# The last 64 rows of two weight matrices as whole rows on 64 partitions

## The chip, the cores and the metric

The kernel runs on one core of one Trainium2 chip. The metric is the time of one execution on the device in microseconds (us). Three executions of the kernel before took 196.46, 196.88 and 197.08 us; the median is 196.88 us. A further execution was taken with the hardware profiler; all durations of instructions and transfers below are from that one.

## The reference

Two branches read the same input x (8 rows of 448) and are mixed by a gate:

```python
q = x @ wq                                  # 8 x 448 times 448 x 4096: 16 heads of 256
scores = q . k * 256**-0.5                  # 8 KV heads, the last 1024 of 4096 cached keys
o = softmax(scores) . v                     # two query heads share one KV head
a = o @ wo                                  # 4096 x 448

y = layernorm(x)
b = gelu(y @ w1 + b1) @ w2 + b2             # 448 -> 1792 -> 448

g = sigmoid((x * gate_w).sum(-1))
out = g * a + (1 - g) * b
```

All tensors are bf16. The keys and values that are read come to 64 MiB; the weights wq, wo, w1 and w2 come to about 10 MiB.

## The kernel before

**Layout of the weights.** The contraction length of wq and w1 is 448 = 3 x 128 + 64. The first 384 rows lie in `wq_sb` and `w1_sb` as three slices of 128 partitions. The last 64 rows (DM to D) lie in `wq_t` and `w1_t` (lines 109 and 112) on all 128 partitions: each row is cut into two halves, and row r's half h lies on partition 2r + h. One partition then holds 4096 B of wq or 1792 B of w1.

Since a partition of these tiles holds only one half of a row, the transposed input must be zero on the partitions of the other half. `halves` (line 261) copies the last 64 columns of x (or y) into every second column of a zeroed tile `x_e` (or `y_e`), once per half, and `transposed` (line 268) turns the three slices and the two halves over on TensorE: five transposes, one copy to `xT` or `yT` with five slices of 8 columns.

**The MLP's first product** (`mlp_up`, line 311) makes 14 blocks of 128 outputs by 8. A block is five matmuls into one PSUM range: three with `w1_sb` (line 321), one with a single row `b1_sb` against ones, which adds the bias (line 325), and one with `w1_t` (line 329). The products for q (line 377) are 96 matmuls with `wq_sb` and 32 with `wq_t`.

**Transfers.** SyncE's queue (SP) issues, in this order, w1 (1344 KB), the tail of w1 (224 KB), w2 (1568 KB), three slices of wq (1024 KB each), the tail of wq (512 KB), and then the stream of K, V and wo: 1024 KB for two batch rows of one KV head, 448 KB for the wo rows of one head. ScalarE's queue (ACT) issues x, b1 and b2 at the start and gate_w later. There are eight semaphores for transfers, used in rotation over both queues, so that a transfer is issued only when the transfer eight places before it has landed whole. K and V have twelve buffers.

**Order.** The order of instructions is the program's own. After the MLP and q, a loop over 64 steps (two per K transfer) transposes the K tile on TensorE (line 407), copies it out of PSUM on VectorE (line 412), multiplies with q (line 433), and, seven steps behind, multiplies the exponentials with V (line 508). The last steps are the V products of the last head, the product with the last wo tile (line 533), the mix (line 577) and two transfers of the output.

Of the kernel before, what the change touches and what calls it, by code (L numbers as in the profile page):

```python
# [9 lines left out]
ALU = mybir.AluOpType  # L10
AXIS = mybir.AxisListType
BF16 = mybir.dt.bfloat16
F32 = mybir.dt.float32
# [3 lines left out]
def kernel(  # L17
# [15 lines left out]
    nc = tc.nc  # L33
    P = nc.NUM_PARTITIONS

    B, Sq, D = A_x.shape
    _, Hkv, Sk, Dh = A_k_cache.shape
    HD = A_wq.shape[1]
    Hq = HD // Dh
    rep = Hq // Hkv  # L40
    W = min(4096, max(256, Sk // 4))
    kv0 = Sk - W
    F = B_w1.shape[1]
    NB = B
    NJ = Dh // P
    TB = 2
    NC = W * TB // P
    HC = NC // TB
    NF = F // P
    R = NB * rep  # L50
    RU = TB * rep
    NBU = NB // TB
    DC = D // P
    DM = DC * P
    TL = D - DM
    HH = HD // 2
    assert Sq == 1 and Dh % P == 0 and W % P == 0 and F % P == 0
    FH = F // 2
    NH = NF // 2
    assert TL * 2 == P and NC * R <= 2 * P and NB % TB == 0 and 3 * 32 <= P and R <= 32 and NF % 2 == 0  # L60
    qscale = float(Dh) ** -0.5
    NU = NBU * Hkv
    NSTEP = NU * TB
# [8 lines left out]
    PT = CP * CT  # L72
    DN = D // CT
# [14 lines left out]
    big = ctx.enter_context(tc.tile_pool(name="big", bufs=1))  # L88
    kvpool = ctx.enter_context(tc.tile_pool(name="kvpool", bufs=NKV))
    ktpool = ctx.enter_context(tc.tile_pool(name="ktpool", bufs=3))  # L90
    consts = ctx.enter_context(tc.tile_pool(name="consts", bufs=1))
    work = ctx.enter_context(tc.tile_pool(name="work", bufs=2))
    ps_kt = ctx.enter_context(
        tc.tile_pool(name="ps_kt", bufs=4, space=bass.MemoryType.PSUM)
    )
# [10 lines left out]
    big.tile([P, PAD], BF16, name="pad")  # L106
    NKH = rep * NJ
    wq_sb = big.tile([P, DC, HD], BF16, name="wq_sb")
    wq_t = big.tile([P, HH], BF16, name="wq_t")
    w1_sb = big.tile([P, DC, F], BF16, name="w1_sb")  # L110
    wo_sb = [big.tile([P, NKH, D], BF16, name=f"wo_sb{g}") for g in range(Hkv)]
    w1_t = big.tile([P, FH], BF16, name="w1_t")
    w2_sb = big.tile([P, NF, D], BF16, name="w2_sb")
    x_sb = consts.tile([NB, D], BF16, name="x_sb")
    gw_sb = consts.tile([NB, D], BF16, name="gw_sb")
    b1_sb = consts.tile([1, F], BF16, name="b1_sb")
    b2_sb = consts.tile([1, D], BF16, name="b2_sb")
    ident = consts.tile([P, P], BF16, name="ident")
    identf = consts.tile([P, P], F32, name="identf")
    onesb = consts.tile([P, P], BF16, name="onesb")  # L120
# [3 lines left out]
    cross = consts.tile([TB, TB, rep], BF16, name="cross")  # L124
    diag = [consts.tile([P, R], BF16, name=f"diag{k}") for k in range(2)]
    qT = consts.tile([P, NJ, Hkv, NB, rep], BF16, name="qT")
    xT = consts.tile([P, DC + 2, NB], BF16, name="xT")
    yT = consts.tile([P, DC + 2, NB], BF16, name="yT")
    x_e = consts.tile([NB, 2, P], BF16, name="x_e")
    y_e = consts.tile([NB, 2, P], BF16, name="y_e")  # L130
    gg = consts.tile([NB, 2], F32, name="gg")
    gg4 = consts.tile([PT, 2], F32, name="gg4")
    bvec = consts.tile([PT, DN], F32, name="bvec")
    bsum = consts.tile([PT, DN], F32, name="bsum")
    res = consts.tile([PT, DN], BF16, name="res")

# [4 lines left out]
    def load(kind, n):  # L141
# [11 lines left out]
            )  # L153
        KV[kind, n] = t

    nc.scalar.dma_start(x_sb[:], xf)
    nc.scalar.dma_start(b1_sb[:], B_b1.rearrange("(o f) -> o f", o=1))
    nc.scalar.dma_start(b2_sb[:], B_b2.rearrange("(o d) -> o d", o=1))
    nc.sync.dma_start(  # L159
        w1_sb[:], B_w1[0:DM, :].rearrange("(p c) n -> p c n", c=DC)  # L160
    )
    nc.sync.dma_start(w1_t[:], B_w1[DM:D, :].rearrange("r (h n) -> (r h) n", h=2))  # L162
    w2_v = w2_sb[:].rearrange("p (h k) n -> p h k n", h=2)
    nc.sync.dma_start(w2_v, B_w2.rearrange("(h p k) n -> p h k n", h=2, k=NH))  # L164
    wq_v = A_wq[0:DM, :].rearrange("(p c) n -> p c n", c=DC)
    for c in range(DC):
        nc.sync.dma_start(wq_sb[:, c, :], wq_v[:, c, :])  # L167
    nc.sync.dma_start(wq_t[:], A_wq[DM:D, :].rearrange("r (h n) -> (r h) n", h=2))

    VU = (SPG + LAG) // TB  # L170
    units = []
# [47 lines left out]
    )  # L219
    for t in diag:  # L220
        nc.gpsimd.memset(t[:], 0.0)
    nc.gpsimd.memset(x_e[:], 0.0)
    nc.gpsimd.memset(y_e[:], 0.0)
    nc.gpsimd.tensor_copy(identf[:], ident[:])
    sel = consts.tile([NB, PT], F32, name="sel")
    nc.gpsimd.tensor_copy(
# [5 lines left out]
    prod = consts.tile([NB, D], F32, name="prod")  # L232
# [7 lines left out]
    y_sb = consts.tile([NB, D], BF16, name="y_sb")  # L240
# [7 lines left out]
        op0=ALU.subtract, op1=ALU.mult,  # L248
# [3 lines left out]
    A_ps = A_bank[0:PT, 0:DN]  # L252
# [4 lines left out]
        rhs=zrow[:].unsqueeze(1).to_broadcast([1, 512 // P, P]),  # L257
        start=True, stop=True, skip_group_check=True,
    )

    def halves(dst, src):
        for h in range(2):
            nc.vector.tensor_copy(
                dst[:, h, :].rearrange("b (r h) -> b r h", h=2)[:, :, h],
                src[:, DM:D],
            )

    def transposed(dst, t, t_e):
        v = t[:, 0:DM].rearrange("b (p c) -> b c p", c=DC)
        parts = [v[:, c, :] for c in range(DC)] + [t_e[:, h, :] for h in range(2)]  # L270
        tp = ps_kt.tile([P, W], BF16, tag="ktp", name="tp")
        for c, part in enumerate(parts):
            nc.tensor.transpose(
                tp[:, c * NB : (c + 1) * NB], part, ident[0:NB, 0:NB]
            )
        nc.vector.tensor_copy(
            dst[:], tp[:, 0 : len(parts) * NB].rearrange("p (c b) -> p c b", b=NB)
        )

    halves(y_e, y_sb)  # L280
    transposed(yT, y_sb, y_e)
    halves(x_e, x_sb)
    transposed(xT, x_sb, x_e)


    def gate_load():
        src = gate_w.rearrange("(o d) -> o d", o=1)
        nc.scalar.dma_start(gw_sb[:], src.to_broadcast([NB, D]))

    def gate():  # L290
        nc.vector.tensor_tensor(prod[:], x_sb[:], gw_sb[:], op=ALU.mult)
        nc.vector.reduce_sum(gsum[:], prod[:], axis=AXIS.X)
        nc.scalar.activation(gth[:], gsum[:], ACT.Tanh, scale=0.5)
        nc.vector.tensor_scalar(
            gg[:, 0:1], gth[:], 0.5, 0.5, op0=ALU.mult, op1=ALU.add
        )
        nc.vector.tensor_scalar(
            gg[:, 1:2], gg[:, 0:1], -1.0, 1.0, op0=ALU.mult, op1=ALU.add
        )

        nc.tensor.matmul(
            A_bank[0:PT, DN : DN + 2], lhsT=sel[:], rhs=gg[:],
            start=False, stop=True, skip_group_check=True,
        )
        nc.vector.tensor_copy(gg4[:], A_bank[0:PT, DN : DN + 2])
        nc.vector.tensor_scalar_mul(bvec[:], bsum[:], gg4[:, 1:2])


    M = {}
# [1 line left out]
    def mlp_up():  # L311
        h_ps = ps_g.tile([P, 512], F32, tag="grp", name="h_ps")
        for h in range(2):
            for k in range(NH):
                o = h_ps[:, (h * NH + k) * NB : (h * NH + k + 1) * NB]

                def cols(w):
                    return w.rearrange("p (q k) -> p k q", k=NH)[:, k, :]

                for c in range(DC):  # L320
                    nc.tensor.matmul(  # L321
                        o, lhsT=cols(w1_sb[:, c, h * FH : (h + 1) * FH]),
                        rhs=yT[:, c, :], start=(c == 0), stop=False,
                    )
                nc.tensor.matmul(
                    o, lhsT=cols(b1_sb[:, h * FH : (h + 1) * FH]),
                    rhs=onesb[0:1, 0:NB], start=False, stop=False,
                )
                nc.tensor.matmul(  # L329
                    o, lhsT=cols(w1_t[:]), rhs=yT[:, DC + h, :],  # L330
                    start=False, stop=True,
                )
        N = NF * NB
        z = consts.tile([P, N], F32, name="z")
        u = consts.tile([P, N], F32, name="u")
        th = consts.tile([P, N], F32, name="th")
        hT = consts.tile([P, N], BF16, name="hT")
        nc.vector.tensor_copy(z[:], h_ps[:, 0:N])  # L338
        nc.vector.tensor_tensor(u[:], z[:], z[:], op=ALU.mult)
        nc.vector.tensor_scalar(u[:], u[:], 0.044715, 1.0, op0=ALU.mult, op1=ALU.add)  # L340
        nc.vector.tensor_tensor(u[:], u[:], z[:], op=ALU.mult)
        nc.scalar.activation(th[:], u[:], ACT.Tanh, scale=0.7978845608028654)
        nc.vector.tensor_scalar(th[:], th[:], 1.0, 0.5, op0=ALU.add, op1=ALU.mult)
        nc.vector.tensor_tensor(hT[:], th[:], z[:], op=ALU.mult)  # L344
        M["hT"] = hT
# [23 lines left out]
    NQ = Hq * NJ  # L369
    for c in range(DC + 1):  # L370
        for k in range(NQ):
            if c < DC:
                w, xs = wq_sb[:, c, k * P : (k + 1) * P], xT[:, c, :]
            else:
                h, kk = divmod(k, NQ // 2)
                w, xs = wq_t[:, kk * P : (kk + 1) * P], xT[:, DC + h, :]
            nc.tensor.matmul(
                q_ps[:, k * NB : (k + 1) * NB],
                lhsT=w,
                rhs=xs,  # L380
                start=(c == 0 and k == 0),
                stop=(c == DC),
                skip_group_check=True,
            )
# [161 lines left out]
    for n in range(LAST):  # L546
# [28 lines left out]
    o_proj(Hkv - 1)  # L575

    nc.vector.scalar_tensor_tensor(  # L577
        res[:], in0=A_ps, scalar=gg4[:, 0:1], in1=bvec[:], op0=ALU.mult, op1=ALU.add
    )
    for j, eng in enumerate((nc.sync, nc.scalar)):  # L580
        eng.dma_start(
# [30 lines left out]
```

## Time and profile before

| what | value |
|---|---|
| median of three executions | 196.88 us |
| the profiled execution's own time | 196.92 us |
| its span, first to last instruction | 195.2 us |
| TensorE, VectorE, ScalarE, GpSimd busy | 164.2, 113.1, 6.4, 2.8 us |
| moved by DMA | 78.14 MB, mean 400 GB/s |
| packets on SP's queue (q1), share of 16 DMA engines over the span | 12688, 95.4% |
| packets on ACT's queue (q10) | 52 |
| packets that bring instructions (q8) | 26 of 16 KB |
| mean granted TensorE clock | 0.768 |

The device time of an execution is some 1.7 us longer than the span, which runs from the first to the last instruction of the program. In lists of groups, `L407 PE MATMUL ktp<-ident,kv x1024` is line 407, engine, operation, the tile written and the tiles read, and the count; PEld is TensorE's weight load. `SPq` and `ACTq` are the queues' issuing instructions. In the windows view the last two numbers of a line are the share of time that the 16 DMA engines were moving packets, and the GB/s.

### The profile page before, as it was taken

What the parts mean: (1) busy time and instruction counts of PE and PEld (TensorE: products, weight loads), DVE (VectorE), ACT (ScalarE), POOL (GpSimd) and SP (SyncE); (2) the same over time, 40 slices, a digit from 0 to 9 for tenths busy, and PEclk for the clock granted to TensorE, in tenths of its full rate; (3) what the DMA queues carried; (4) which work ended last, traced back from release to release, by engine and by line L of the source; (5) the groups of instructions that cost most, each with busy time, mean ns of one, the idle gap of its engine ahead of it and who ended that gap; (6) DMA issues with size and microseconds to landing.
All of it is one profiled execution on the core that took longest, in us unless ns stands there. A gap on an engine that the chain in (4) does not pass through costs nothing.

```text
span 195.2 us, 7355 instructions
## 1 busy us (share of the span) xinstructions
PE 164.2 (84%) x3417; PEld 153.6 (79%) x3417; DVE 113.1 (58%) x255; ACT 6.4 (3%) x13; POOL 2.8 (1%) x16
## 2 busy tenths in 40 slices
PE   2677799988899796958999898988898989989752
PEld 1565799988899796957999797978897989989541
DVE  3122189996477653764559674964586646766401
ACT  5000000000000000010000000000000000000000
POOL 5000000000000000000000000000000000000000
PEclk9999889997569855585569996995599655699555
DMA  6999999999999999999999999999999999999940
GB/s 215 412 426 425 425 413 426 426 423 420 421 426 422 417 425 426 425 417 431 423 423 419 422 425 428 418 421 418 425 430 417 421 425 430 426 420 425 394 176 5
DMA packets 12769, 78.14 MB, mean 400 GB/s; under 512 B 1330, under 2 KB 3523, under 8 KB 4164
## 3 DMA queue, kind: packets, MB, share of 16 engines
q1 hardware_dynamic: 12688, 77.67, 95.4%
q8 instruction: 26, 0.43, 0.8%
q10 hardware_dynamic: 52, 0.02, 0.0%
q14 instruction: 3, 0.02, 0.0%
HBM read 77.68 MB, written 0.01 MB: 398 GB/s over the span
## 4 chain that ended last, share of the span: by engine, by line
DMA 91%; PE 6%; SPq 1%; issue 0%; DVE 0%
DMA kv<-in_A_k_cache_dram 47%; DMA kv<-in_A_v_cache_dram 19%; DMA wo_sb<-in_A_wo_dram 18%; DMA wq_sb<-in_A_wq_dram 7%; PE ktp L407 4%; PE grp L433 1%; PE A_bank L533 0%; PE grp L508 0%; SPq L167 0%; PE grp L422 0%; SPq L164 0%; DVE res L577 0%; SPq L159 0%; SPq L162 0%; SPq L148 0%
## 5 line engine op out<-in xcount | busy, mean ns | idle before, releaser
L412 DVE COPY kt<-ktp 128x1024 bf16<-128x1024 bf16 x128 | 84.4, 687 | 44.4 <-PE ktp L407 43.9
L407 PE MATMUL ktp<-ident,kv 128*128 128x128 bf16 x1024 | 89.0, 257 | 7.9 <-DMA kv<-in_A_k_cache_dram 6.7
L407 PEld LDWEIGHTS <-kv 128*128 128x128 bf16 x1024 | 78.0, 118 | 10.9 <-DMA kv<-in_A_k_cache_dram 7.9
L508 PE MATMUL grp<-e,kv 128*128 128x4 bf16 x1024 | 35.6, 166 | 2.6 <-DMA kv<-in_A_v_cache_dram 2.5
L508 PEld LDWEIGHTS <-kv 128*128 128x128 bf16 x1024 | 32.6, 101 | 5.6 <-DMA kv<-in_A_v_cache_dram 2.8
L433 PE MATMUL grp<-qT,kt 128*128 128x4 bf16 x1024 | 36.6, 166 | 0.3 <-DVE kt L412 0.2
L433 PEld LDWEIGHTS <-kt 128*128 128x128 bf16 x1024 | 34.6, 100 | 1.8 <-issue 0.6
L482 ACT ACTIVATE e<-grp 128x256 bf16<-128x256 f32 x8 | 3.1, 383 | 161.8 <-PE grp L475 161.8
L491 PE MATMUL A_bank<-zs,onesf 128*128 128x16 f32 x16 | 3.6, 299 | 4.5 <-DVE zs L487 4.5
L491 PEld LDWEIGHTS A_bank<-zs,onesf 128*128 128x128 f32 x16 | 2.8, 218 | 5.1 <-DVE zs L487 5.1
L533 PE MATMUL A_bank<-wo_sb,ot 128*8 128x224 bf16 x64 | 5.5, 305 | 0.8 <-DMA wo_sb<-in_A_wo_dram 0.5
L321 PE MATMUL h_ps<-yT,w_sb 128*128 128x8 bf16 x42 | 4.2, 195 | 1.2 <-DMA w_sb<-in_B_w_dram 1.2
L495 DVE RECIPROCAL rz<-A_bank 128x16 f32<-128x16 f32 x8 | 2.1, 258 | 5.4 <-PE A_bank L491 5.4
L519 DVE TENSOR_TENSOR ot<-grp,rz 128x32 bf16<-128x32 f32 x8 | 1.5, 186 | 6.4 <-PE grp L508 6.4
L487 DVE TENSOR_REDUCE zs<-e 128x16 f32<-128x256 bf16 x8 | 4.8, 602 | 0.0
L353 PE MATMUL b_ps<-w_sb,hT 128*8 128x224 bf16 x28 | 2.8, 388 | 2.4 <-DVE b_ps L349 2.4
L338 DVE COPY z<-h_ps 128x112 f32<-128x112 f32 x1 | 0.3, 275 | 7.7 <-PE h_ps L329 7.7
L321 PEld LDWEIGHTS <-w_sb 128*128 128x128 bf16 x42 | 3.6, 152 | 1.3 <-DMA w_sb<-in_B_w_dram 1.3
L475 PE MATMUL grp<-diag,onesb 128*128 128x256 bf16 x8 | 2.5, 308 | 2.2 <-DVE diag L469 1.9
L353 PEld LDWEIGHTS <-hT 128*8 128x8 bf16 x28 | 1.8, 121 | 3.0 <-DVE hT L344 2.2
L446 DVE TENSOR_REDUCE pm<-grp 128x16 f32<-128x256 f32 x8 | 3.3, 415 | 0.6 <-PE grp L433 0.6
L533 PEld LDWEIGHTS <-ot 128*8 128x8 bf16 x64 | 2.6, 93 | 1.3 <-issue 0.4
(82 smaller groups left out, 53.6 us busy)
## 6 DMA issues: line engine op xcount, KB each, us to landing
kv<-in_A_k_cache_dram SPq DMA_DIRECT2D x32, 1024.0 KB, 18.3
kv<-in_A_v_cache_dram SPq DMA_DIRECT2D x31, 1024.0 KB, 18.3
wo_sb<-in_A_wo_dram SPq DMA_DIRECT2D x8, 448.0 KB, 18.3
wq_sb<-in_A_wq_dram SPq DMA_DIRECT2D x3, 1024.0 KB, 12.1
w_sb<-in_B_w_dram SPq DMA_DIRECT2D x1, 1568.0 KB
w_sb<-in_B_w_dram SPq DMA_DIRECT2D x1, 1344.0 KB, 5.9
kv<-in_A_v_cache_dram SPq DMA_DIRECT2D x2, 512.0 KB, 19.8
wq_t<-in_A_wq_dram SPq DMA_DIRECT2D x1, 512.0 KB, 14.5
```

What stands on the lines that cost most here:

```text
L321: nc.tensor.matmul(o, lhsT=cols(w1_sb[:, c, h * FH : (h + 1) * FH]), rhs=yT[:, c, :], start=(c == 0), stop=False,)
L353: nc.tensor.matmul(b_ps[CP * j : CP * j + NB, 0:DN], lhsT=M["hT"][:, k * NB : (k + 1) * NB] if k < NF else onesb[0:1, 0:NB], rhs=w2_sb[:, ...
L407: nc.tensor.transpose(ktp[:, c * P : (c + 1) * P], K[:, h * HC + c, j * P : (j + 1) * P], ident[:],)
L412: nc.vector.tensor_copy(kt[:, j, :], ktp[:])
L433: nc.tensor.matmul(G[g][:, s : s + RU], lhsT=kt[:, j, c * P : (c + 1) * P], rhs=qT[:, j, g, bu * TB : (bu + 1) * TB, :].rearrange("p t i - ...
L446: nc.vector.reduce_max(pm[:], G[g][:, S0 : S0 + NC * R].rearrange("p (c r) -> p r c", r=R), axis=AXIS.X,)
L475: nc.tensor.matmul(G[g][:, S0 : S0 + NC * R].rearrange("p (c r) -> p c r", c=NC), lhsT=onesb[:], rhs=diag[g % 2][:].unsqueeze(1).to_broadc ...
L482: nc.scalar.activation(e[:], G[g][:, S0 : S0 + NC * R], ACT.Exp)
L487: nc.vector.reduce_sum(zs[:], E[g][:].rearrange("p (c r) -> p r c", r=R), axis=AXIS.X)
L491: nc.tensor.matmul(zc, lhsT=onesf[:], rhs=zs[:], start=False, stop=True, skip_group_check=True)
L508: nc.tensor.matmul(G[g][:, o : o + RU], lhsT=V[:, cc, :].rearrange("p (q j) -> p j q", j=NJ)[:, j, :], rhs=E[g][:, cc * R + bu * RU : cc * ...
L533: nc.tensor.matmul(A_bank[CP * j : CP * j + NB, 0:DN], lhsT=ot[:].rearrange("p j (b i) -> p j i b", i=rep)[:, h, i, :], rhs=wo_sb[g][:, k, ...
```

## The change

The last 64 rows of wq and w1 are placed as whole rows on partitions 0 to 63, one row on each. A helper `low` loads them in two transfers of 32 rows. The source of such a transfer is written with an outer dimension of 8: row 8r + i of the 32 goes to partition 4i + r, and `transposed` puts the columns of x and y into the same order before the transpose. The tail of wq stays on SP's queue, the tail of w1 goes to ACT's. b1 is loaded as a 65th row of `w1_t`, and the transposed y has a row of ones there, so that the bias comes with the tail's matmul; the 14 matmuls of line 325 fall away. There are four transposes for x and four for y, in place of five, and two copies out of PSUM in place of one. `gw_sb` now lies in `w1_sb`, and `bvec` in `bsum`. SP issues as many transfers before the first K as before (w1, w2, three slices of wq, two of its tail); ACT issues five in place of three.

```diff
-    wq_t = big.tile([P, HH], BF16, name="wq_t")
+    wq_t = big.tile([P, HD], BF16, name="wq_t")
-    w1_t = big.tile([P, FH], BF16, name="w1_t")
+    w1_t = big.tile([P, F], BF16, name="w1_t")
-    gw_sb = consts.tile([NB, D], BF16, name="gw_sb")
-    b1_sb = consts.tile([1, F], BF16, name="b1_sb")
+    gw_sb = w1_sb[0:NB, 0, 0:D]
...
+    def low(eng, dst, w):
+        for h in range(TL // 32):
+            eng.dma_start(
+                dst[32 * h : 32 * (h + 1), :],
+                w[DM + 32 * h : DM + 32 * (h + 1), :].rearrange("(r i) n -> i r n", i=8),
+            )
+
     nc.scalar.dma_start(x_sb[:], xf)
-    nc.scalar.dma_start(b1_sb[:], B_b1.rearrange("(o f) -> o f", o=1))
+    nc.scalar.dma_start(w1_t[TL : TL + 1, :], B_b1.rearrange("(o f) -> o f", o=1))
     nc.scalar.dma_start(b2_sb[:], B_b2.rearrange("(o d) -> o d", o=1))
...
-    nc.sync.dma_start(w1_t[:], B_w1[DM:D, :].rearrange("r (h n) -> (r h) n", h=2))
+    low(nc.scalar, w1_t, B_w1)
...
-    nc.sync.dma_start(wq_t[:], A_wq[DM:D, :].rearrange("r (h n) -> (r h) n", h=2))
+    low(nc.sync, wq_t, A_wq)
...
-    nc.gpsimd.memset(x_e[:], 0.0)
-    nc.gpsimd.memset(y_e[:], 0.0)
+
+    nc.vector.memset(yT[TL : TL + 1, DC, :], 1.0)
...
+        nc.vector.tensor_copy(
+            t_e[:].rearrange("b (h i r) -> b h i r", i=8, r=4),
+            t[:, DM:D].rearrange("b (h r i) -> b h i r", i=8, r=4),
+        )
...
                 nc.tensor.matmul(
-                    o, lhsT=cols(b1_sb[:, h * FH : (h + 1) * FH]),
-                    rhs=onesb[0:1, 0:NB], start=False, stop=False,
-                )
-                nc.tensor.matmul(
-                    o, lhsT=cols(w1_t[:]), rhs=yT[:, DC + h, :],
-                    start=False, stop=True,
+                    o, lhsT=cols(w1_t[0 : TL + 1, h * FH : (h + 1) * FH]),
+                    rhs=yT[0 : TL + 1, DC, :], start=False, stop=True,
                 )
...
-                h, kk = divmod(k, NQ // 2)
-                w, xs = wq_t[:, kk * P : (kk + 1) * P], xT[:, DC + h, :]
+                w, xs = wq_t[0:TL, k * P : (k + 1) * P], xT[0:TL, DC, :]
```

More of the change, by code (lines that the diff above doesn't have):

```diff
@@ L55 @@
     TL = D - DM
-    HH = HD // 2
     assert Sq == 1 and Dh % P == 0 and W % P == 0 and F % P == 0
@@ L59 @@
     NH = NF // 2
-    assert TL * 2 == P and NC * R <= 2 * P and NB % TB == 0 and 3 * 32 <= P and R <= 32 and NF % 2 == 0
+    assert TL % 32 == 0 and TL < P and NC * R <= 2 * P and NB % TB == 0 and 3 * 32 <= P and R <= 32 and NF % 2 == 0
     qscale = float(Dh) ** -0.5
@@ L126 @@
     qT = consts.tile([P, NJ, Hkv, NB, rep], BF16, name="qT")
[L127 to L130, printed above, removed]
+    xT = consts.tile([P, DC + 1, NB], BF16, name="xT")
+    yT = consts.tile([P, DC + 1, NB], BF16, name="yT")
+    x_e = consts.tile([NB, TL], BF16, name="x_e")
+    y_e = consts.tile([NB, TL], BF16, name="y_e")
     gg = consts.tile([NB, 2], F32, name="gg")
     gg4 = consts.tile([PT, 2], F32, name="gg4")
-    bvec = consts.tile([PT, DN], F32, name="bvec")
     bsum = consts.tile([PT, DN], F32, name="bsum")
@@ L259, with transposed @@
     )
[L261 to L265, printed above, removed]
-            )
[L268 to L274, printed above, removed]
-            )
+    def transposed(dst, t, t_e):
+        nc.vector.tensor_copy(
+            t_e[:].rearrange("b (h i r) -> b h i r", i=8, r=4),
+            t[:, DM:D].rearrange("b (h r i) -> b h i r", i=8, r=4),
+        )
+        v = t[:, 0:DM].rearrange("b (p c) -> b c p", c=DC)
+        tp = ps_kt.tile([P, W], BF16, tag="ktp", name="tp")
+        for c in range(DC):
+            nc.tensor.transpose(
+                tp[:, c * NB : (c + 1) * NB], v[:, c, :], ident[0:NB, 0:NB]
+            )
+        nc.tensor.transpose(
+            tp[0:TL, DC * NB : (DC + 1) * NB], t_e[:], ident[0:NB, 0:NB]
+        )
         nc.vector.tensor_copy(
-            dst[:], tp[:, 0 : len(parts) * NB].rearrange("p (c b) -> p c b", b=NB)
+            dst[:, 0:DC, :], tp[:, 0 : DC * NB].rearrange("p (c b) -> p c b", b=NB)
         )
-    halves(y_e, y_sb)
+        nc.vector.tensor_copy(dst[0:TL, DC, :], tp[0:TL, DC * NB : (DC + 1) * NB])
     transposed(yT, y_sb, y_e)
-    halves(x_e, x_sb)
     transposed(xT, x_sb, x_e)
@@ L287, in gate_load @@
         src = gate_w.rearrange("(o d) -> o d", o=1)
-        nc.scalar.dma_start(gw_sb[:], src.to_broadcast([NB, D]))
+        nc.scalar.dma_start(gw_sb, src.to_broadcast([NB, D]))
     def gate():
-        nc.vector.tensor_tensor(prod[:], x_sb[:], gw_sb[:], op=ALU.mult)
+        nc.vector.tensor_tensor(prod[:], x_sb[:], gw_sb, op=ALU.mult)
         nc.vector.reduce_sum(gsum[:], prod[:], axis=AXIS.X)
@@ L305, in gate @@
         nc.vector.tensor_copy(gg4[:], A_bank[0:PT, DN : DN + 2])
-        nc.vector.tensor_scalar_mul(bvec[:], bsum[:], gg4[:, 1:2])
+        nc.vector.tensor_scalar_mul(bsum[:], bsum[:], gg4[:, 1:2])
     M = {}
@@ L325, in mlp_up @@
                 nc.tensor.matmul(
-                    o, lhsT=cols(b1_sb[:, h * FH : (h + 1) * FH]),
-                    rhs=onesb[0:1, 0:NB], start=False, stop=False,
-                )
-                nc.tensor.matmul(
-                    o, lhsT=cols(w1_t[:]), rhs=yT[:, DC + h, :],
-                    start=False, stop=True,
+                    o, lhsT=cols(w1_t[0 : TL + 1, h * FH : (h + 1) * FH]),
+                    rhs=yT[0 : TL + 1, DC, :], start=False, stop=True,
                 )
@@ L577 @@
     nc.vector.scalar_tensor_tensor(
-        res[:], in0=A_ps, scalar=gg4[:, 0:1], in1=bvec[:], op0=ALU.mult, op1=ALU.add
+        res[:], in0=A_ps, scalar=gg4[:, 0:1], in1=bsum[:], op0=ALU.mult, op1=ALU.add
     )
```

## The prediction

> **What bounds the kernel now.** I read the page's slices and queues first, then the chain that ended last, then the windows of the last 13 us, then the start's timeline.
>
> ```profile
> DMA  6999999999999999999999999999999999999940
> ...
> q1 hardware_dynamic: 12688, 77.67, 95.4%
> q8 instruction: 26, 0.43, 0.8%
> ...
> DMA 91%; PE 6%; SPq 1%; issue 0%; DVE 0%
> ```
>
> The 16 DMA engines are busy in every slice from the first to the 38th, and 91% of the chain is transfers. TensorE follows: over the whole span its K transposes waited 6.7 us in 9 waits for K. So engine work counts only where it delays the stream, and the question is what the change does to the transfers.
>
> ```profile
> 182.00:185.00 3.00, 2.64 (x58) 2.09 (x57) 0.92 (x3) 0.38 (x1) 0.00 (x0) 0.50 0.99 406
> 185.00:187.00 2.00, 1.39 (x37) 1.30 (x34) 0.26 (x1) 0.00 (x0) 0.00 (x0) 0.50 0.57 230
> 187.00:189.00 2.00, 1.01 (x32) 0.93 (x32) 0.00 (x0) 0.00 (x0) 0.00 (x0) 0.50 0.50 194
> 189.00:190.00 1.00, 0.59 (x16) 0.51 (x16) 0.00 (x0) 0.00 (x0) 0.00 (x0) 0.50 0.29 112
> 190.00:191.40 1.40, 0.61 (x18) 0.61 (x20) 0.19 (x1) 0.00 (x0) 0.00 (x0) 0.50 0.05 20
> ```
>
> The windows' last two columns (DMA share, GB/s) say that the end is not a matter of bandwidth. From 185 us only half of the DMA engines still move, from 190 us one or two. The chain ends on the slowest of them:
>
> ```profile
> 174.03 17.30 DMA wo_sb<-in_A_wo_dram
> 191.33 0.04 issue
> 191.37 0.93 PE A_bank L533 x8
> 192.30 0.02 issue
> 192.32 0.44 DVE res L577
> ```
>
> Every large transfer is spread evenly over all 16 engines, so the kernel ends when the engine with the most work is through. The trace holds each packet (queue, start, duration, bytes) and each of the 16 steps of a transfer's semaphore, one per DMA engine. The 16 steps of the last wo transfer came at 184.98, 185.05, 185.12, 185.41, 185.47, 185.50, 185.71, 186.85, then 189.63 to 189.89 (six), 190.66 and 191.33 us. Eight engines are 3 to 6 us ahead of the other eight.
>
> **Why eight are late.** An undisturbed engine takes an 8192 B packet every 306 ns, so the steps of one engine in successive K and V transfers lie 2453 ns apart, and each engine (I call it a lane, since the trace doesn't number them) can be followed through the run by that spacing. Eight lanes show jumps of 1410 to 1460 ns, which fall on the 26 packets of 16 KB of queue q8 (instructions): each lane is hit every eighth fetch, 3 times each, two of them 4 times (3 x 1.41 = 4.2 us and 4 x 1.41 = 5.6 us, which is the spread above). The two with four hits are those that end at 191.33 and 190.66. The other eight have none (two of them have other jumps, of 588 and twice 840 ns).
>
> The Trainium skill, "Runtime: NRT & Kernel Launch", section "Instruction fetch mechanics", says that a sequencer fetches its program in 16 KiB blocks of 256 instructions through its own DMA queue, and that crossing a boundary is mostly hidden. The 26 packets agree; "hidden" holds for TensorE here, not for the DMA engine that carries the block, which loses 1.41 us. Were it hidden there too, all lanes would end together and the sum would be +1.75 us, 198.7.
>
> **Which lanes the new transfers use.** The transfer amid the stream that has an outer dimension of 8 is gate_w (8 rows of 896 B, moved at 63.3 to 63.5 us). Its eight packets fall on eight different lanes, each set back by 36 to 44 ns. Six of these are lanes without instruction fetches (they end at 184.98 to 186.85), and two are lanes with them: one of the six with three fetches (189.7), and the one that ends at 190.66 with four. I take it that the new transfers, whose outer dimension is 8 too, use these eight. The bound on the other side is all 16 lanes, as with the 128-row transfers.
>
> The skill's "DMA: Bandwidth & Descriptors", section "Why a DMA increments its semaphore by 16 and not by 1", says that a transfer runs on the largest number up to 16 that divides the slowest dimensions of both sides, on the lowest-numbered engines: here 8, as gate_w shows. Its section "Rules for kernel authors" warns of this: an outermost dimension under 16 confines the transfer to so many engines. By its advice (16 engines) the sum would be zero.
>
> **The sum, per lane.** Old tails: 8 packets of 1792 B every 71 ns (0.57 us) and a wq tail whose steps lie 1.25 us after those of the transfer before it: 1.82 us on each of 16 lanes. New tails: 8 packets of 3584 B (b1's own packet of that size took 140 ns, so 137 apart: 1.10 us), 8 of 8192 B (2.45 us) and four semaphore packets of 6 ns: 3.57 us on eight lanes, nothing on the rest. So eight lanes gain 1.75 us of work, eight lose 1.82. The last landings become:
> - lane at 191.33, not among the eight: 189.51
> - lane at 190.66, among them: 192.41
> - lane at 189.7, among them: about 191.5
> - the six early ones among them: at most 186.85 + 1.75 = 188.60
>
> The last landing moves from 191.33 to 192.41, +1.08 us. What follows (eight matmuls 0.93, the mix 0.44, the output's transfer) is unchanged. 196.92 + 1.08 = 198.0 us; the profiled execution is 0.04 us above the median of the three, so against the median too it is 198.0.
>
> **The rest of the change, priced at nothing, and its cover.**
>
> ```profile
> 1.99 1.28 ACT L244 ACT_TABLE_LOAD   x1 [1.99 <-issue]
> 5.52 0.18 DVE L276 COPY xT<-tp 128x40 bf16<-128x40 bf16 x1 [0.28 <-PE tp L273]
> 6.73 0.32 PE L321 MATMUL h_ps<-yT,w_sb 128*128 128x8 bf16 x3 [1.24 <-DMA w_sb<-in_B_w_dram]
> 21.26 0.96 PE L377 MATMUL q_ps<-xT,wq_t 128*128 128x8 bf16 x32
> 23.54 3.20 PE L407 MATMUL ktp<-ident,kv 128*128 128x128 bf16 x32 [1.33 <-DMA kv<-in_A_k_cache_dram]
> 26.89 0.55 PE L433 MATMUL grp<-qT,kt 128*128 128x4 bf16 x16
> ```
>
> - ACT issues two more transfers (0.23 to 0.59 us each by its three rows) before its table load at 1.99, so rstd and yT come 0.5 to 1.2 us later: yT from 5.0 to at most 6.2, still before w1 lands (6.68).
> - The tail of w1 behind x, b1 and b2 on ACT's queue: b1, issued at 1.43, moved only at 5.09, and its semaphore packet one SP packet later (5.63). Ten packets in turn with SP's (0.24 to 0.40 us each plus 0.14) from 5.1 us end at 9 to 10.5, where the old tail landed at 7.2. The 14 blocks wait for it from the first one on. Each block sheds a matmul of line 325 (0.15 us of pace, 2.1 us for 14), so q comes between 0 and 1.5 us later than 22.2. TensorE's next work waits for K until 23.5 and needs qT only at 26.9: covered. Without that cover it would cost up to 1.5 us, once.
> - K's first issues (7.07 and 7.75) now wait for these two transfers' semaphores, until 9 to 10.5. SP's queue then still holds wq, which ends at 18.4: no engine runs dry. A later start costs only if it passes 18 us.
> - SP issues one instruction less ahead of w2 (0.41 us) and two in place of one for wq's tail (0.33 each): behind queued packets, nothing.
> - GpSimd sheds two memsets (0.30 each), VectorE sheds two copies of about 0.15 and gains two of up to 0.18 and a memset of 0.06; TensorE sheds two transposes: all before 6.7 us. bvec in bsum is the same instruction; gate_w still lands before its use.
> - TensorE's program is 32 rows shorter. The last fetch, at 186.60, moves later by 32 instructions, half of the 32-matmul burst (1.0 us) that ran before it: to about 187.1. The lane it hits is busy until 192.4, so it still counts.
>
> **Rivals.**
> 1. *Faster:* the eight lanes are all free of fetches. I could have lost a lane where two run within some ns of each other. For: the end is set by late lanes alone, so any byte that leaves them is a gain. Against: the two gate_w lanes were 1.41 us behind at 62 us, before it came, and kept their 2453 ns on both sides. Then the last landing is 191.33 - 1.82 = 189.51: 195.1 us. It decides if no lane with four fetches is among the eight and the lane at 189.7 isn't either.
> 2. *The other eight:* 191.33 + 1.75: 198.7 us. Against: gate_w.
> 3. *The last fetch comes too late or doesn't come:* the 190.66 lane has three hits, ends at 192.41 - 1.41 = 191.0, and the lane at 191.5 sets the end: +0.13, 197.05 us. Against: at 186.6 there were 148 TensorE instructions to run.
> 4. *No change:* the transfers spread over 16 lanes after all: 196.9 us.
>
> **How the numbers follow.** Forecast 60%, rival 1 20%, rival 2 6%, rival 3 8%, rival 4 6%. Some 0.3% (0.59 us) is what a measurement of this kernel tells from no change. Faster 0.20 (rival 1), same 0.14 (3 and 4), slower 0.66. The range leaves out rival 1 alone: from rival 4 less the 0.4 us by which the fastest execution fell short of the median, 196.5, to rival 2 and 0.2 us above, 198.9. The forecast's own range, with 0.3 us for the packet times and 0.4 for the executions, is 197.4 to 198.6.
>
> **What would show it.** Right: the last wo transfer's steps split with one lane near 192.4 alone, one near 191.5, most late ones near 188, early ones near 187; the tail's packets 3584 and 8192 B on eight lanes; DMA share of about 0.5 from 187 on. Wrong: the last landing at 189.5, or a span with an idle DMA slice in the first 25 us.

## The result

Over 20 executions the kernel after has a median of 197.53 us, against 196.81 us for the kernel before on the same chip. The ratio is 1.0045, with a 95% interval of 1.0025 to 1.0065: the change makes the kernel slower by about half a per cent. The forecast was 198.0 us, slower.

The median hides something that the forecast did not contain. The times of the kernel before lie in one group (196.46 to 197.58). Those of the kernel after lie in two, and the median falls into the gap between them:

| kernel | executions | lower group | upper group |
|---|---|---|---|
| before | 20 | all, 196.46 to 197.58 | none |
| after | 20 | ten, 196.90 to 197.22 | ten, 197.85 to 199.10 |

The granted TensorE clock doesn't separate the two groups: it is 0.757 to 0.795 in the lower and 0.746 to 0.805 in the upper.

The profiled execution (198.41 us, span 196.7) is one of the upper group. The page's slices, queues and chain:

```profile
DMA  6999999999999999999999999999999999999920
...
q1 hardware_dynamic: 12480, 77.44, 94.4%
q8 instruction: 26, 0.43, 0.8%
q10 hardware_dynamic: 132, 0.25, 0.4%
...
DMA 75%; PE 20%; DVE 4%; issue 1%
```

Up to the 38th slice the DMA engines are as busy as before; in the 39th their share fell from 4 to 2 tenths. Queue q10 has the tail of w1 and b1. The 26 instruction packets are still there. The chain now has TensorE in it here and there, because it follows the buffers' release back; its last links show what counts:

```profile
175.65 17.27 DMA wo_sb<-in_A_wo_dram
192.96 0.93 PE A_bank L532 x8
193.91 0.44 DVE res L576
```

The last landing is at 192.92 us (191.33 before), and what follows it is what it was. The windows of the end:

```profile
182.00:185.00 3.00, 2.10 (x41) 1.50 (x40) 1.40 (x6) 0.38 (x1) 0.00 (x0) 0.50 0.92 376
185.00:187.00 2.00, 1.89 (x52) 1.78 (x50) 0.26 (x1) 0.00 (x0) 0.00 (x0) 0.50 0.85 343
187.00:189.00 2.00, 1.01 (x32) 0.93 (x32) 0.00 (x0) 0.00 (x0) 0.00 (x0) 0.50 0.31 118
189.00:190.00 1.00, 0.00 (x0) 0.00 (x0) 0.00 (x0) 0.00 (x0) 0.00 (x0) 0.50 0.11 37
190.00:191.40 1.40, 0.59 (x16) 0.50 (x16) 0.00 (x0) 0.00 (x0) 0.00 (x0) 0.50 0.11 45
```

Read the last two columns against those of before. From 185 to 187 us the DMA share rose from 0.57 to 0.85: most lanes now end together, at 186.8 to 187.9. From 187 on it fell from 0.50 to 0.31, and from 189.2 on two lanes are left (0.11 is about two sixteenths). The 16 steps of the last wo transfer say the same lane by lane: 183.47, 183.64, then twelve from 186.83 to 189.21, then 191.51 and 192.92 us. The last two lanes carry both a share of the tails and instruction fetches, one of them three and the other four.

The edits that were priced at nothing stayed hidden. The timeline of the start:

```profile
1.97 1.45 ACTq L157 DMA_DIRECT2D w_t<-in_B_w_dram  x2
...
3.45 1.28 ACT L250 ACT_TABLE_LOAD   x1 [3.45 <-issue]
...
6.27 0.14 DVE L284 COPY yT<-tp 64x8 bf16<-64x8 bf16 x1
...
6.73 0.32 PE L325 MATMUL h_ps<-yT,w_sb 128*128 128x8 bf16 x3
...
8.76 0.61 SPq L145 DMA_DIRECT2D kv<-in_A_k_cache_dram  x1
...
10.62 0.19 PE L329 MATMUL h_ps<-yT,w_t 65*128 65x8 bf16 x1 [3.57 <-DMA w_t<-in_B_w_dram]
...
22.51 0.50 DVE L388 TENSOR_SCALAR qT<-q_ps 128x128 bf16<-128x128 f32 x2 [3.04 <-PE q_ps L376]
...
23.61 3.33 PE L406 MATMUL ktp<-ident,kv 128*128 128x128 bf16 x32 [1.14 <-DMA kv<-in_A_k_cache_dram]
```

ScalarE's table load begins at 3.45 instead of 1.99, yT is whole at 6.41, before the first product with w1 at 6.73, the first K is issued at 8.76 instead of 7.07, the MLP waits 3.57 us for the tail of w1, and VectorE starts qT at 22.51 (22.25 before). The K transposes begin at 23.61 (23.54 before), still on a wait for K.

### The profile page after: what moved, and what is told of

It is laid out like the page before. It is cut to its first block, busy times and chain, and to the rows that moved or that the text cites. A ratio compares the mean times of both kernels' runs of the same rounds, so it can differ in the third digit from the quotient of the medians.

```text
span 196.7 us, 7327 instructions
## 1 busy us (share of the span) xinstructions
PE 161.0 (82%) x3401; PEld 150.4 (76%) x3401; DVE 113.7 (58%) x256; ACT 6.4 (3%) x13; POOL 2.3 (1%) x14
## 4 chain that ended last, share of the span: by engine, by line
DMA 75%; PE 20%; DVE 4%; issue 1%
DMA kv<-in_A_k_cache_dram 47%; PE ktp L406 12%; DMA kv<-in_A_v_cache_dram 10%; DMA wo_sb<-in_A_wo_dram 9%; DMA wq_sb<-in_A_wq_dram 6%; DMA w_sb<-in_B_w_dram 3%; PE grp L507 3%; PE grp L432 2%; DVE kt L411 2%; PE A_bank L532 2%; DVE zs L486 1%; PE A_bank L490 1%; PE grp L474 0%; DVE diag L468 0%; DVE res L576 0%
## 5 line engine op out<-in xcount | busy, mean ns | idle before, releaser
L406 PE MATMUL ktp<-ident,kv 128*128 128x128 bf16 x1024 | 87.9, 255 | 9.0 <-DMA kv<-in_A_k_cache_dram 8.8
L490 PE MATMUL A_bank<-zs,onesf 128*128 128x16 f32 x16 | 4.2, 341 | 3.9 <-DVE zs L486 3.9
L490 PEld LDWEIGHTS A_bank<-zs,onesf 128*128 128x128 f32 x16 | 3.4, 264 | 4.5 <-DVE zs L486 4.5
L532 PE MATMUL A_bank<-wo_sb,ot 128*8 128x224 bf16 x64 | 6.2, 336 | 0.7 <-DMA wo_sb<-in_A_wo_dram 0.5
L329 PE MATMUL h_ps<-yT,w_t 65*128 65x8 bf16 x14 | 2.7, 194 | 3.6 <-DMA w_t<-in_B_w_dram 3.6
L329 PEld LDWEIGHTS <-w_t 65*128 65x128 bf16 x14 | 2.1, 151 | 3.6 <-issue 3.6
```

The costliest lines, as they stand in the source:

```text
L329: nc.tensor.matmul(o, lhsT=cols(w1_t[0 : TL + 1, h * FH : (h + 1) * FH]), rhs=yT[0 : TL + 1, DC, :], start=False, stop=True,)
L406: nc.tensor.transpose(ktp[:, c * P : (c + 1) * P], K[:, h * HC + c, j * P : (j + 1) * P], ident[:],)
L490: nc.tensor.matmul(zc, lhsT=onesf[:], rhs=zs[:], start=False, stop=True, skip_group_check=True)
L532: nc.tensor.matmul(A_bank[CP * j : CP * j + NB, 0:DN], lhsT=ot[:].rearrange("p j (b i) -> p j i b", i=rep)[:, h, i, :], rhs=wo_sb[g][:, k, ...
```

## The experiments

Two theories stood at the start, and a third came after the first runs. **L (lanes)**: the end is set by the sum of tail bytes and instruction fetches on the slowest DMA engine. **P (prologue)**: the time is lost at the start, by the tail on ACT's queue or the later issue of K. **S (shared partitions)**, the later one: what matters is which partitions a DMA engine writes.

### The kernel after, again

> The changed kernel once more. Theory L (lanes): the end is set by the DMA engine with the most work; the tails lie on eight engines, two of which also carry instruction fetches (1.41 us each), and which engines get a fourth fetch differs from execution to execution. Then the times fall into two groups, near 197.0 us (no fourth fetch among the eight: lane 189.7 + 1.75, +0.13 us) and near 198.4 us (one of the two has four: +1.1 to +1.6 us), and hardly between; in the profile the last wo transfer ends on a lane that has the tails and fetches. Theory P (prologue): the later tail of w1, the longer queue of ScalarE and the later first K cost a steady amount; the times form one group near 197.5 us.

Measured: six executions at 196.44 to 196.92 us, six at 197.71 to 198.43; median 197.31, ratio 1.003 [1.0009, 1.005]. The two groups are real. This profiled execution (196.83) fell into the lower one:

```profile
175.49 15.87 DMA wo_sb<-in_A_wo_dram
191.40 0.93 PE A_bank L532 x8
```

The last landing is 1.56 us earlier than in the profiled execution above, of the very same kernel. The traces differ in one thing that explains it: on which lane the first instruction fetch falls. The packets of q8 last a few per cent longer or shorter by lane, in a sequence that repeats every eight, so their durations are a fingerprint. The first eight of three traces, in ns:

```
before (196.92 us)              947 879 887 942 931 921 961 965
after (198.41 us)               951 885 878 936 933 921 960 961
after, again (196.83 us)        967 954 886 886 936 931 922 960
```

I number the positions by the first two rows, 0 to 7; in the third row the sequence begins at position 7. Followed by their spacing and jumps, the two lanes that carry both fetches and tails are positions 1 and 2. With 26 = 3 x 8 + 2 fetches, the first two lanes of the sequence get a fourth: positions 0 and 1 in the first two traces, 7 and 0 in the third. So in the execution of 198.41 us a lane with a tail has four fetches, and in that of 196.83 us none has: its two last lanes end at 191.11 and 191.36, with three each. The start was at 0, 1, 2, 4, 5 or 7 in the traces of this study. The kernel before doesn't show it in its time: with equal tails on all lanes, it is all one which lane gets the fourth. Its own trace starts at 0 and has its last landing at 191.33; the run of the next section, whose lanes carry the same bytes, starts at 2 and has it at 191.09.

### The tail of w1 on ACT's queue alone

```diff
-    nc.sync.dma_start(w1_t[:], B_w1[DM:D, :].rearrange("r (h n) -> (r h) n", h=2))
+    nc.scalar.dma_start(w1_t[:], B_w1[DM:D, :].rearrange("r (h n) -> (r h) n", h=2))
```

> The kernel before with w1's tail issued on ScalarE's queue instead of SyncE's, all else as it was (half rows on 128 partitions, 16 lanes). Theory L: the lanes carry what they did: 196.8 us, ratio 0.999 to 1.002, although w1's tail lands 1 to 3 us later. Theory P: the later tail delays the prologue: 197.5 us.

Measured, as an edit of the kernel before: 196.74 us (196.60 to 197.04), ratio 0.9997 [0.9988, 1.0005], last landing 191.09. The tail lands later here (the first product with it runs at 9.5 us instead of 7.3) and costs nothing. K is issued as early as before in this run (7.05). That a later issue of K costs nothing either is shown by the execution of 196.83 us above: its first K is issued at 8.73, its qT begins at 22.70, and its time is that of the kernel before. So P is refuted.

### The tails on 16 lanes, and on eight lanes but as half rows

The first is the kernel after with each tail in one plain transfer of 64 rows:

```diff
-        for h in range(TL // 32):
-            eng.dma_start(
-                dst[32 * h : 32 * (h + 1), :],
-                w[DM + 32 * h : DM + 32 * (h + 1), :].rearrange("(r i) n -> i r n", i=8),
-            )
+        eng.dma_start(dst[0:TL, :], w[DM:D, :])
...
```

The columns of x and y are put in the natural order to match.

> The change with one edit undone: each tail is one transfer of 64 rows without the outer dimension of 8 (natural row order), so that it spreads over 16 engines; whole rows on partitions 0 to 63, b1 as the 65th row, w1's tail on ScalarE's queue all stay. Theory L: each lane has 4 packets of 3584 B and 4 of 8192 B, 1.8 us as before the change; 196.7 to 197.0 us in one group, ratio 0.998 to 1.002, last landing near 191.3. Theory P: the prologue is that of the changed kernel, so 197.5 us, ratio 1.003 to 1.005.

The second is the kernel before (128 half rows) with an outer source dimension of 8:

```diff
-    nc.sync.dma_start(wq_t[:], A_wq[DM:D, :].rearrange("r (h n) -> (r h) n", h=2))
+    nc.sync.dma_start(wq_t[:], A_wq[DM:D, :].rearrange("r (h n) -> (r h) n", h=2).rearrange("(q i) n -> i q n", i=8))
...
```

The tail of w1 is edited likewise, and the zero-padded inputs are permuted to match.

> The kernel before with the one edit alone: half rows on 128 partitions, all on SyncE's queue as before, but the source has an outer dimension of 8 (the zero-padded inputs are permuted to match). Theory L: 16 packets of 1792 B and 16 of 4096 B on eight lanes, 3.6 us in place of 1.8, none on the rest: as the changed kernel, two groups near 197.0 and 198.4 us, mean ratio 1.002 to 1.007. Theory P: as before, 196.8 us.

Measured: 199.47 us (199.40 to 200.15), ratio 1.0149 [1.0135, 1.0163], and 201.10 us (200.72 to 203.09), ratio 1.0235 [1.0205, 1.0265]. Both theories missed, by 2 to 4 us, and on the slow side. The trace of the 16-lane kernel shows where, in the windows of the start:

```profile
4.00:12.00 8.00, 2.85 (x44) 2.56 (x45) 1.25 (x8) 1.40 (x2) 0.00 (x0) 1.00 1.01 371
12.00:19.00 7.00, 4.59 (x68) 3.39 (x67) 2.04 (x8) 0.30 (x1) 0.00 (x0) 1.00 1.03 423
19.00:22.00 3.00, 2.20 (x88) 2.11 (x85) 0.12 (x1) 0.00 (x0) 0.00 (x0) 1.00 0.97 218
```

The same windows of the kernel after:

```profile
4.00:12.00 8.00, 2.46 (x37) 2.20 (x38) 1.32 (x8) 2.31 (x3) 0.00 (x0) 1.00 1.00 419
19.00:22.00 3.00, 3.00 (x117) 2.98 (x116) 0.38 (x1) 0.00 (x0) 0.00 (x0) 1.00 1.03 426
```

The DMA engines are busy all the time in both, but from 19 to 22 us, while the tail of wq and the first K arrive, they move 218 GB/s instead of 426, and from 4 to 12 us, with the tail of w1, 371 instead of 419. The 8192 B packets took a mean of 578 ns there, against 312 in the same window of the kernel after. In the kernel with half rows on eight lanes the 4096 B packets took 362 to 376 ns from 19 to 26 us (159 in the kernel before) and the 8192 B packets beside them 769 from 19 to 22 us. A tail laid out in this way slows itself and the transfers next to it. The traces don't show which partitions a lane writes. If a transfer's rows are dealt out to its lanes in order, half of the lanes of the plain transfer of 64 rows write partitions that in the large transfers belong to others. Theory S: two engines on one group of partitions share its rate.

The Trainium skill, "SBUF — State Buffer", section "Door 1: The DMA port swizzle (why `[64,N]` ≈ `[32,N]`)", says that bandwidth depends on how many of 16 ports the partitions reach, and that a partition p and p + 32 are on the same port while p + 64 is not. The run with 64 rows on 16 lanes agrees with it (578 ns a packet in place of 312). By its table the kernel after's mapping, row 8r + i on partition 4i + r, gives each of eight engines a port of its own; the trace agrees there too, with 312 ns.

### S against the lanes: four lanes, wrong partitions

The kernel after, with the tail of wq on four lanes, so that one lane writes eight neighbouring partitions, and the tail of w1 as above in one transfer of 64 rows:

```diff
-                w[DM + 32 * h : DM + 32 * (h + 1), :].rearrange("(r i) n -> i r n", i=8),
+                w[DM + 32 * h : DM + 32 * (h + 1), :].rearrange("(r i) n -> i r n", i=4),
...
-    low(nc.scalar, w1_t, B_w1)
+    nc.scalar.dma_start(w1_t[0:TL, :], B_w1[DM:D, :])
...
```

> The changed kernel with wq's tail in transfers with an outer dimension of 4 and w1's tail spread over 16. Theory L: the tail of wq (1.25 us on each of 16 lanes before) lies on four lanes (4.9 us). If these four are free of instruction fetches they end at 185.5 + 3.66 = 189.1 (190.5 for one with two other jumps), and the rest at 191.33 - 1.25 = 190.1: the end is 1.25 us earlier than before, 195.6 us, and in one group, because the fetches then always fall on lanes without the tail. If one of the four carries fetches: 189.7 + 3.66 or 190.7 + 3.66, 199 to 200 us. Theory P: 197.5 us as the changed kernel.

Measured: 201.54 us (201.27 to 203.37), ratio 1.0263 [1.0231, 1.0294]. From 19 to 22 us the 8192 B packets took 575 ns, from 22 to 30 us 480:

```profile
19.00:22.00 3.00, 2.30 (x87) 2.21 (x83) 0.07 (x1) 0.00 (x0) 0.00 (x0) 1.00 1.06 240
22.00:26.00 4.00, 0.00 (x0) 0.00 (x0) 0.00 (x0) 0.00 (x0) 0.00 (x0) 1.00 1.00 223
26.00:30.00 4.00, 0.99 (x32) 0.94 (x32) 0.40 (x2) 0.00 (x0) 0.00 (x0) 1.00 0.99 315
```

As the rows are laid out, each of the four lanes has eight partitions of its own, so the tail doesn't collide with itself but with the large transfers beside it. The profiled execution is the longest of the six (203.37 us) and ends on TensorE: its last wo transfer has landed at 195.89, and the last products begin at 197.84.

The last wo steps say something of the lanes besides: four lanes are early (189.16 to 190.43), the next ends at 193.23. Of the eight lanes without fetches four are thus outside this tail and four are in it: the four lanes that a transfer with an outer dimension of 4 uses carry none of the packets of q8.

### More bytes on the same eight lanes, and on all

To the kernel after 459 KB more are added (the tail of w1 twice more, into tiles that the last wo transfers overwrite later), once in the form of the change and once on all 16 lanes:

```diff
+    for g in (Hkv - 2, Hkv - 1):
+        low(nc.sync, wo_sb[g][:].rearrange("p k n -> p (k n)"), B_w1)
```

> The changed kernel with two more loads of 64 whole rows of 3584 B (w1's last rows once more, into wo tiles that are filled again later), each as the change does it: two transfers of 32 rows with an outer dimension of 8. 459 KB more on the same eight lanes: 16 packets of 137 ns each, 2.2 us. Theory L: both groups of the changed kernel's times move by +2.2 us, to about 199.2 and 200.6 us. By bytes alone at 424 GB/s it would be +1.1 us. Theory S (two DMA engines that write to the same group of partitions halve each other) adds nothing here: engine i writes partitions 4i to 4i+3 and 32+4i to 35+4i, as in the large transfers; the packets of 3584 B take 140 ns.

```diff
+    for g in (Hkv - 2, Hkv - 1):
+        nc.sync.dma_start(
+            wo_sb[g][:].rearrange("p k n -> p (k n)")[:, 0:FH],
+            B_w1[DM:D, :].rearrange("r (h n) -> (r h) n", h=2),
+        )
```

> The same 459 KB more, but as half rows of 1792 B on 128 partitions, 16 lanes: 16 packets of 71 ns on each lane, 1.14 us. Theory L: both groups of the changed kernel's times move by +1.1 us, to 198.1 and 199.5 us, half of what the same bytes cost on eight lanes.

Measured: 199.79, 200.62, 200.89 and 201.23 us on eight lanes (ratio 1.0194 [1.0173, 1.0215]; 199.2 and 200.6 expected), 197.99, 198.41, 198.43 and 199.59 on sixteen (1.0093 [1.0067, 1.012]; 198.1 and 199.5 expected). The profiled execution with eight ends on two lanes at 194.87 and 195.15: its fetches start at position 1, so that both lanes with a tail have four, and 195.15 is 192.92 + 2.23 us, the dose that L expected (2.2). The one with sixteen starts at position 7, like the lower one of the kernel after, and its last landing is 192.80, 1.44 above 191.36 (1.14 expected). So the same bytes cost more on eight lanes than on sixteen. The last links of the chain with eight:

```profile
177.77 17.38 DMA wo_sb<-in_A_wo_dram
195.19 0.93 PE A_bank L534 x8
```

### The tail of wq on six lanes

The kernel before, with 48 rows of the tail of wq in two transfers with an outer dimension of 6 and 16 rows, cut by columns into three, with one of 4, on the partitions that belong to these lanes. If all six were free of fetches, the end would be earlier.

```diff
+    for h in range(2):
+        nc.sync.dma_start(
+            wq_t[32 * h : 32 * h + 24, :],
+            A_wq[DM + 24 * h : DM + 24 * (h + 1), :].rearrange("(r i) n -> i r n", i=6),
+        )
...
```

> The kernel before, with wq's tail alone as whole rows, placed so that the lowest six DMA engines carry it and each writes its own partitions: 24 rows on partitions 0 to 23 and 24 on 32 to 55, both with an outer dimension of 6, and 16 rows as a second slice on partitions 0 to 15 with an outer dimension of 4 (in wo tiles that are filled later), multiplied by 32 more matmuls; w1's tail stays on 128 partitions. Theory L and S together: four lanes carry 3.72 us, two 2.46, the other ten nothing, in place of 1.25 on each. If the lowest six are free of instruction fetches, the lanes with fetches end at 191.33 - 1.25 = 190.1 at the latest, the four at 185.7 + 2.5 = 188.2 (189.4 for one with other jumps): 195.6 us in one group, ratio 0.993 to 0.995. If one of the four carries fetches: 189.7 + 2.5 or more, 197.8 us or above. Theory P (the prologue's order costs): no gain over 196.8, since more transfers stand ahead of the first K.

Measured: nine executions at 196.38 to 196.72 us, three at 197.60 to 198.26; median 196.61, ratio 1.0005 [0.9987, 1.0024]. The gain expected did not come. The 8192 B packets stay at 309 ns (S), but the last wo steps of the profiled execution (198.26) end with 188.38, 189.51, 189.92 and, alone, 192.58: one of the two lanes that were added to the four carries fetches, and in this execution four of them.

### Without the fourth fetch

If the groups come from the fourth fetch, they go when no lane has one. TensorE's program is cut by 544 rows, so that 24 packets are left, three to each of the eight lanes wherever they start. The edit is the same in both kernels:

```diff
+        nj = 1 if n < 34 else NJ
...
-            for j in range(NJ):
+            for j in range(nj):
...
-                    stop=(j == NJ - 1),
+                    stop=(j == nj - 1),
```

> The kernel after, with the second half of the scores' contraction (the matmuls with j = 1) left out in the first 34 steps, so that TensorE's program is 544 rows shorter and ends before its 25th block of 16 KB; the output is not the reference's. Theory L (lanes): 24 fetches fall on eight lanes exactly three times each, wherever they start, so no lane has a fourth. The two lanes that carry both fetches and a tail end near 191.5 us (192.92 less 1.41, and 191.51): 196.9 to 197.3 us, in one group, with nothing near 198.4. Theory G (the two groups have another source than the fetches): the two groups some 1.2 us apart stay.

> The kernel before with the same matmuls left out. Theory L: the two lanes with a fourth fetch, which end before's execution at 191.33, lose it, and the last landing is that of the three-hit lanes, 189.9: 195.4 to 195.6 us, 1.4 us less than the kernel before and 1.5 to 1.8 less than the kernel after with 24 fetches. Theory G: a fetch costs the stream nothing, and the time stays at 196.8.

Measured: the kernel after has nine executions at 196.67 to 197.13 us and three at 197.64, 198.05 and 198.80; its last landings are 191.04 and 191.25 us (191.5 expected). The kernel before has nine at 195.31 to 195.57 and one at 197.13; median 195.48, ratio 0.994 [0.9923, 0.9958]. The cut also takes work from TensorE, but that is not what saves the time: the same cut leaves the lower group of the kernel after where it was. So 1.3 us of the kernel before's time is the fourth fetch on two lanes, and with three on each the change costs 1.4 us in the median (196.88 to 195.48; 1.5 to 1.8 expected).

The stray executions have another cause in the one that was profiled (before, 197.13). Its last landing is early, at 189.82, but its chain doesn't end on a transfer:

```profile
186.97 0.84 PE A_bank L534 x8
187.81 0.52 PE grp L509 x16
188.33 0.45 PE A_bank L492 x2
188.78 2.55 PE grp L509 x96
191.60 0.93 PE A_bank L534 x8
```

The first number is the start, the second the duration: TensorE is late and does its last 96 products with V without a pause, after the DMA engines have finished. In the other kernel the three stray executions have the three lowest granted clocks of the twelve (0.722, 0.738 and 0.741; the nine others 0.749 to 0.785). That these three have the same cause is likely and not shown, since none of them has a trace. So the cut was moved to the last 34 steps, which takes work from TensorE near the end and leaves 24 fetches:

```diff
-        nj = 1 if n < 34 else NJ
+        nj = 1 if n >= 30 else NJ
```

> The kernel after with the second half of the scores' contraction left out in the last 34 steps instead of the first 34: the same 24 fetches, and less work for TensorE near the end; the output is not the reference's. In the run with the first 34 steps cut, nine of twelve executions were at 196.67 to 197.13 us and three at 197.6 to 198.8, with the three lowest granted clocks (0.722 to 0.741). Theory L (lanes) together with E (those three were TensorE coming late at a low clock): nearly all executions at 196.6 to 197.2, none near 198.4. Theory G (the two groups of the kernel after are not made by the fetches): about half, or at least a quarter, of the executions stay at 197.7 to 198.8, also at clocks above 0.75.

Measured: all eleven executions at 196.68 to 197.35 us, median 196.93, ratio 1.0007 [0.9998, 1.0016]; the last landings are 191.23 and 191.38. Of 32 executions of the kernel after with 26 fetches, 16 were at 197.71 or more; of these eleven, none. The two groups are made by the fourth fetch.

```profile
175.58 15.81 DMA wo_sb<-in_A_wo_dram
191.43 0.93 PE A_bank L533 x8
192.38 0.44 DVE res L577
```

### The tail of wq on four lanes, right partitions

The kernel before, with the tail of wq alone on the four lanes that carry no fetches of q8, two rows to a partition, on partitions 0 to 15 and 32 to 47. The tile lies in that of the last five wo's, and GpSimd zeroes it first; the q products have 32 matmuls more.

```diff
+    nc.gpsimd.memset(wq_t[0:64, :], 0.0)
+    for h in range(2):
+        nc.sync.dma_start(
+            wq_t[32 * h : 32 * h + 16, :],
+            A_wq[DM + 32 * h : DM + 32 * (h + 1), :].rearrange("(q i) n -> i q n", i=4),
+        )
...
```

> The kernel before with wq's tail alone changed: its 64 rows go to the four lowest engines, which carry no TensorE fetches, 16 rows of 8192 B to each, two rows to a partition, on the partitions that the same engines write in 128-row transfers (0 to 15 and 32 to 47). w1's tail and b1 stay as they were before. Theory L: the lanes with fetches lose the old tail's 1.25 us and gain nothing: last landing 191.33 - 1.25 = 190.1; the four lanes end at 185.0 to 186.85 less 1.25 plus 4.9 = 188.7 to 190.5. So 195.6 to 196.0 us in one group, whichever lane the fetches start on, and 27 fetches (64 more rows) cost nothing more than 26. Theory S (shared partitions): 8192 B packets stay near 309 ns. Rival: no gain, 196.8, if the time goes by bytes or by the start.

Measured: ten executions at 196.05 to 196.34 us, and 197.35 and 197.95; median 196.23, ratio 0.9978 [0.9959, 0.9996]. It is the only whole kernel that beats the one before, and by little. (Of the two stray executions the one of 197.35 us has the same span as the others, 194.5, and the one of 197.95 a longer one, 196.2; neither has a trace, and their cause stays open.) The same four lanes as in the run with eight neighbouring partitions, with the right ones:

```profile
19.00:22.00 3.00, 1.32 (x16) 1.03 (x18) 1.16 (x5) 0.30 (x1) 0.00 (x0) 1.00 1.03 434
22.00:26.00 4.00, 4.00 (x105) 3.17 (x102) 0.38 (x1) 0.00 (x0) 0.00 (x0) 1.00 1.01 422
```

434 and 422 GB/s in place of 240 and 223, and 309 to 311 ns a packet in place of 575 to 582. Both runs split the tail's source over four lanes in the same way. So it is the partitions, and not the number of lanes, that cost the rate.

The last three lanes end at 189.75, 190.01 and 190.71 us, and the third sets the time:

```profile
q8 instruction: 27, 0.44, 0.8%
q14 instruction: 3, 0.02, 0.0%
...
174.84 15.87 DMA wo_t<-in_A_wo_dram
190.75 0.93 PE A_bank L546 x8
```

The first two are lanes with four fetches, as expected (190.1). The third is not a lane with fetches of q8: it is one of the four that carry the tail. Its first K lands at 25.3 us, as that of the other three does (20.2 to 20.8 on the twelve lanes without the tail), and its steps show two jumps of 0.97 us, each following a packet of 8 KB of a second instruction queue, q14 (moved at 46.38 and 119.57 us). The other three lanes of the tail have none and end at 188.4 to 189.0. The expectation had this lane as the one with other jumps, and priced it at 190.5.

## Why the prediction was right, and where it was wrong

- **What bounds the kernel** was right: the lane with the most work, not the bytes in all. The doses show it (the same bytes moved the last landing by 2.23 us on eight lanes and by 1.44 on sixteen), and the runs with 24 fetches show the share of the fetches.
- **A fetch costs its lane 1.41 us**: confirmed in size. Taking the fourth away took 1.3 us from the time of the kernel before. The Trainium skill calls the cost of crossing a block "mostly hidden" ("Runtime: NRT & Kernel Launch", section "Instruction fetch mechanics"). On the DMA engine that carries the block it isn't, and in this kernel, which the DMA engines bound, the time shows it.
- **The eight lanes from gate_w** were right: the tails' packets fall on the same eight, two of them with fetches.
- **The tail's cost, 3.57 us on eight lanes in place of 1.82 on all**, held, because the mapping avoids shared partitions. The forecast named no such condition; the two runs without that order of rows came out 2 to 4 us above what was expected of them.
- **"Lane at 190.66, among them: 192.41" is the step that failed.** It took the lane with four fetches for a property of the kernel. The four fetches were counted in one execution of before; which lanes get them changes from execution to execution, and in about half of them (16 of 32) none of the eight lanes has four. Then both lanes have three and set the end together: 191.11 and 191.36 measured, where the sum gives 191.5 and, without the fourth fetch, 191.0; the time was 196.83 us. That is rival 3's outcome (197.05 us) for another reason: the last fetch isn't late or missing, it lands elsewhere. Rival 3 had 8%.
- **Forecast 198.0** describes the upper group alone (197.85 to 199.10, and 197.71 to 198.43 in the second series). That the median of all, 197.53, comes near it is luck twice over: the one trace of before that was read began its fetches at position 0, where a trace that began at 7 would have led the same sum to rival 3's 197.05, and the executions of the kernel after split ten to ten. In the profiled execution the lane with four landed at 192.92, 0.5 later than the sum. That lane's third wq slice had already landed about 0.5 us later than the sum has it; this is read from one trace, and where in the first transfers it was lost stays open.
- **Rivals 1, 2 and 4** (all eight free of fetches; the other eight lanes; no change): refuted by the lanes of the tail's packets.
- **The edits at nothing** cost nothing, with two times a little off: yT was whole at 6.41 (at most 6.2 forecast), still ahead of w1's first product, and the last fetch came at 188.1 (187.1 forecast), while its lane was still busy. The tail of w1 landed at 8.75 and 10.49 (9 to 10.5), K's first issues were at 8.76 and 10.50, and qT began 0.26 us later (0 to 1.5). The executions of the lower group contain all of these edits: their median is 197.05 us (196.81 before) in the first series and 196.76 (196.77 before) in the second.
- **The "other jumps"** on two lanes, which the prediction left without a cause, come in the steps that follow the three packets of 8 KB of queue q14 (at 40.95, 109.36 and 123.95 us in the trace of before). For the forecast this made no difference, since these lanes end early; in the run on four lanes, right partitions, one of them sets the end.

## What to carry to other kernels

When every large transfer is spread evenly, look at the steps of the last transfer's semaphore: the kernel ends with the DMA engine that carries the most, and instruction fetches count as part of that work. Place an uneven transfer on the engines that end early, and have each engine write the partitions that it writes in the large transfers; else the tail and its neighbours run at about half the rate. Before taking one trace's lane as fixed, look at the spread of the times: a median between two groups is the time of no execution.

## What the runs showed of the hardware

- The lane of the first instruction fetch differs between executions: positions 0 and 7 of eight in two traces of the kernel after, and 0, 1, 2, 4, 5 and 7 over all traces. From there the fetches of q8 go round the same eight lanes. Why the start differs stays open.
- A second instruction queue, q14, brings three packets of 8 KB in every run, on two of the lanes that q8 leaves alone; they cost these lanes 0.59 us and twice 0.84 us (the prediction's reading of before).
- Amid the even stream the duration of an instruction packet depends on its lane (879 to 967 ns in the rows above), steadily enough to name the lane by it.
- A tail on partitions that, by theory S, other engines write in the large transfers nearly doubles the packets' time (309 to 575 ns and more for 8192 B), while the DMA share stays at 0.97 to 1.06: the share of busy time doesn't show this loss, only the GB/s does.
- In two profiled executions TensorE was the end, not a transfer: its last products began 1.8 us after the last landing in the kernel before with 24 fetches (189.82 to 191.60) and 1.9 us after it in the run on four lanes with neighbouring partitions (195.89 to 197.84).
